# Transposes behind a burst, exponentials held back inside a block, loads held ahead of the sums of x: attention and MLP on one core

## The chip, the cores and the metric

The kernel runs on one core of a Trainium2 chip. The core has five engines with instruction queues of their own: TensorE (PE; PEld is its weight load), VectorE (DVE), ScalarE (ACT), GpSimd (POOL) and SyncE (SP), and 16 DMA engines that all queues share. The metric is the device time in microseconds of one execution, lower being better.

## The reference

Attention over 8 batches, 12 heads, 448 tokens and 64 columns a head, followed by a two-layer MLP on the 3584 x 768 result:

```python
attn = softmax(q @ k.T / sqrt(64))           # per batch and head
x = (attn @ v).transpose(0, 2, 1, 3).reshape(3584, 768)
h = x @ w_in                                  # 768 x 2048
out = maximum(0.01 * h, h) @ w_out            # 2048 x 768, float32
```

All inputs and the output are float32 in HBM; the kernel computes in bf16 with float32 sums.

## The kernel before

**Units, chunks, rows.** A unit is a pair of heads of one batch; there are 48, six to a batch. Its q and k are cast to bf16 (`cast`, lines 164 to 174: on POOL, a tile `qkb` with three buffers) and transposed into `qkT` (four buffers). Units below 15 are transposed on TensorE (`transposes`, eight small transposes at line 268 into a PSUM bank and a VectorE copy at line 274); from unit 15 on, SP issues a DMA transpose (`dma_transposes`, line 251). A unit has four chunks of 112 keys, numbered through (chunk 4u + c). For a chunk TensorE makes the scores of both heads (line 285), ScalarE their exponentials e (line 294). A burst is three chunks in a row, in the three PSUM slots. Rows of a unit (`rows`, line 802) multiply the exponentials by v; VectorE divides (lines 808 and 809) and x is turned into `xT`, by a DMA transpose on SP, or, for units 9, 10 and 11 (`X_PE`), on TensorE by `settle_x` some time later (lines 331 and 332).

**The MLP.** Tokens are worked in seven ranges (`cuts`): 640, 512, 512, 512, 512, 384 and 512. The first range is made in a head (448 tokens, 16 blocks of the hidden dimension, numbered from 0; line 366 makes a block in two halves of three matmuls) and a neck (its other 192 tokens, line 662, which take the k-steps of the first two groups except the last before anything else). Each block ends in a Prelu on ScalarE into h (lines 642 and 687). Two PSUM banks, taken in turn by `next_bank`, serve the blocks and the transposes. The later ranges are made by `hidden` (line 483), which works with sums and differences of x and of the weights: `mix_x_part` (line 430, VectorE) makes those of x, in place and in `x_mix`, in two parts, once the rows that they need have been turned. `second(i)` multiplies h of range i by `w_out` (lines 555 and 620), joins on VectorE (lines 560 and 563) and stores. Between its matmuls it places the bursts and rows for later ranges, and the sums of x of the next range, on VectorE's queue too.

**What sets the order.** All engines run what the program writes in the order in which it is written; nothing is moved at run time. Head, neck and `second` call a planner, `place`, with a small model of TensorE's time (`now`), of ScalarE's (`act`) and of when each slot is free. At each step it may place a due transpose, a burst (if all three slots will be free), or rows. In head and neck a step is called full when a block has just been closed, and not full when half of one is done. `lazy` is the number of a burst's exponentials that are not issued at once but after the next block's Prelu (`settle`); no rows are placed while such ones are owed. Behind a burst of head and neck, `feed` places POOL's casts and loads.

In `second` and `hidden`, `advance` places at each of its steps a DMA transpose, a cast of q and k, a cast of v and a load, as far as each may go. A load (`load_soft`, line 143) fetches two units of one of q, k and v by a DMA that POOL issues and that casts on the way; a load from unit u may go once unit u - 3, the last one in the buffer that it overwrites, has been cast. Before the change it is tried at every second step (`tick`). `mix_x_part`'s first part is placed from 7 us of the model behind the last row but one that the next range needs, the second part 7 us behind the last one (`fresh`, `summed`).

Of the kernel before, what the change touches and what calls it, by code (L numbers as in the profile page):

```python
# [16 lines left out]
def kernel(  # L17
# [16 lines left out]
    NSC = S // SC  # L34
# [3 lines left out]
    NU = B * HP  # L38
# [610 lines left out]
    def neck(outs):  # L649

        n = cuts[1] - HEAD
        at = place_of(HEAD)
        ms = [x + y for x in range(0, MH, 2) for y in (0, MH)]
        held = {}

        def part2(m, kks):
            fresh = m not in held
            if fresh:
                held[m] = next_bank()
            for j in range(2):  # L660
                for kk in kks:
                    nc.tensor.matmul(  # L662
                        held[m][:, j * n:(j + 1) * n], w_in_sb[:, kk, ts(m + j, P)], xT[:, kk, at:at + n],
                        start=(fresh and j == 0 and kk == 0), stop=(kk == KD - 1), skip_group_check=True,
                    )

        assert all(u == need[1] - 1 for u, _ in owed_x), owed_x
        def after(x):
            for _ in range((0, 0, 2, 3, 4, 3, 0, 0)[x]):
                next(outs)  # L670

        for m in ms[:2]:
            part2(m, range(KD - 1))
        yield 4 * (KD - 1) * n / 2400, False
        for x, m in enumerate(ms):
            if x < 2:
                assert rows_done >= need[1], rows_done
                settle_x()
                part2(m, (KD - 1,))
                if x:  # L680
                    after(x - 1)
            else:
                part2(m, range(KH))
                after(x - 1)
                yield 2 * KH * n / 2400, False
                part2(m, range(KH, KD))
            nc.scalar.activation(
                h[:, m:m + 2, HEAD:cuts[1]], held.pop(m)[:, :2 * n].rearrange("p (m t) -> p m t", m=2), AX.Prelu, alpha=0.01
            )
            settle(1)  # L690
            yield 2 * (KH if x > 1 else 1) * n / 2400, True
        model["free"][id(slots[0])] = model["now"] + 1.5
        transposes(NPE - 1, next_slot()[:, 0])
        after(len(ms) - 1)
# [71 lines left out]
    chunk = 4 * HP + 3  # L766
    rows_done = HP
    to = {"pe": HP + 2, "turn": NPE, "q": HP + 4, "cast": HP + 4, "v": HP + 4, "load": [HP + 8] * 3}
    tick = 0

    def advance():
        nonlocal tick
        tick += 1
        u = to["turn"]
        if u < min(NU, chunk // NSC + NQ, to["cast"]):
            dma_transposes(u)
            to["turn"] += 1
        u = to["cast"]
        if u < min(NU, to["turn"] + 2, to["load"][0], to["load"][1]):
            cast(u, (0, 1))  # L780
            to["cast"] += 1
        u = to["v"]
        if u < min(NU, rows_done + NV, to["load"][2]):
            cast(u, (2,))
            to["v"] += 1
        if tick % 2 == 0:
            x = min(range(3), key=lambda x: to["load"][x])
            u = to["load"][x]
            if u < NU and u - 3 < (to["cast"], to["cast"], to["v"])[x]:
                load_soft(u, 2, (x,))  # L790
                to["load"][x] += 2
# [42 lines left out]
    X_PE = (HP + 3, HP + 4, HP + 5)  # L834
    owed_x = []

    def settle_x(now=None):
        while owed_x and (now is None or owed_x[0][1] <= now and model["free"].get(id(slots[0]), 0.0) <= now + 0.05):
            model["free"][id(slots[0])] = model["now"] + 1.0
            model["now"] += 0.3  # L840
            x_transposes(owed_x.pop(0)[0], next_slot()[:, 0])
# [43 lines left out]
    def place(i, want, soon=0, full=True, calm=True, first=False, lazy=0, keen=NU, cap=NU):  # L885

        free, ready = model["free"], model["ready"]
        done, state = 0, 0
        while True:
            settle_x(model["now"])  # L890
            now = model["now"]
            last = divmod(chunk + 2, NSC)[0]
            blocked = rows_done <= min(last, NU - 1) - NE
            u = rows_done
            whole = u < chunk // NSC
            at = [free.get(id(x), 0.0) for x in slots]
            u = to["pe"]
            if full and max(want, soon) > done and u <= min(last, NPE - 1) and state == 0:
                transposes(u)
                to["pe"] += 1  # L900
                state = 1
                model["now"] += 0.45
                continue
            if want > done and state < 2 and turned(last) and not blocked and len(slots) == 3 and all(
                x <= now + 0.05 + 0.2 * j for j, x in enumerate(at)
            ):
                state = 2
                order = list(slots)
                start = chunk
                burst(lazy)  # L910
                if first:
                    feed(start // 3)
                done += 1
                for x, t in enumerate(order[:chunk - start]):
                    model["act"] = max(model["act"], now + 0.45 + 0.2 * x) + 0.8
                    free[id(t)] = model["act"] + (0.3, 0.15 + 0.5 * (lazy > 1), 0.15 + 0.5 * lazy)[x]
                    if (start + x) % NSC == NSC - 1:
                        ready[(start + x) // NSC] = model["act"] + 0.1
                model["now"] = now + 0.78
                continue  # L920
            u = to["pe"]
            if first and full and state == 0 and u < min(NPE - 1, to["cast"] - 1) and u <= chunk // NSC + 1 and model["act"] <= now + 0.6:
                transposes(u)
                to["pe"] += 1
                state = 1
                model["now"] += 0.45
                continue
            u = rows_done
            if calm and whole and not (lazy and late) and at[0] <= now + 0.05 and ready.get(u, 0) <= now + 0.05 and (
                u <= (chunk + 5) // NSC - NE or u < keen  # L930
            ) and u < cap:
                t = slots[0]
                rows()
                if first:
                    pay()
                model["now"] = now + 1.08
                free[id(t)] = now + 2.33
                continue
            return done

    def second(i):

        x_sums = [mix_x_part(i + 1, slice(0, 2)), mix_x_part(i + 1, slice(2, 3))] if i + 1 < NR else []
        fresh, summed = [None, None], [i + 1 == NR] * 2
        left = plan[i]
        for c in range(len(spots(i)[1])):
            whole = c < plain(i)
            for x, _ in enumerate((plain_pair if whole else block_pair)(i, c)):
                fine = 1 if whole else 2
                if x % (2 * fine) == 0:  # L950
                    advance()
                if c or x:
                    model["now"] += 0.65 / fine
                left -= place(i, left, calm=whole or x not in (1, 2), keen=need[min(i + 2, NR)], cap=NU if all(summed) else need[i + 2])
                if whole and x in (1, 3, 5, 7):
                    mix_h(i, x - 1)
                if whole and x in (8, 9, 11, 13, 15):
                    next(outs)
                if i == 0 and c and x % 4 == 2:
                    next(ins, None)  # L960
                for y in range(2):
                    if fresh[y] is None and i + 1 < NR and rows_done >= need[i + 2] - 1 + y:
                        fresh[y] = model["now"] + 7.0
                for y, todo in enumerate(x_sums if x % fine == 0 else ()):
                    if fresh[y] is not None and fresh[y] <= model["now"] and not summed[y]:
                        summed[y] = next(todo, 0) is not None
                        if not summed[y]:
                            break
# [10 lines left out]
    for steps, aims, cost in ((head(ins), early, 0.55), (neck(outs), goals, 0.5)):  # L979
        groups = 0  # L980
        base = len(early) if aims is goals else 0
        for used, full in steps:
# [2 lines left out]
                groups += 1  # L985
                model["act"] = max(model["act"], model["now"]) + cost
            soon = base + sum(x <= groups + 1 for x in aims) - done if full else 0
            done += place(0, base + sum(x <= groups for x in aims) - done, soon, first=True, lazy=2 if aims is goals else 1, full=full, keen=NU if aims is goals or groups > 14 else 0)
    settle()
    assert done == len(early) + len(goals), (done, chunk, rows_done)  # L990
    assert to["pe"] == NPE - 1, to
# [5 lines left out]
    for _ in outs:  # L997
        pass
    for i in range(1, NR):
        for step, _ in enumerate(hidden(i)):  # L1000
            advance()
            if step % 4 == 2 and NSC * (rows_done + 1) <= chunk:
# [33 lines left out]
```

## Time and profile before

| what | value |
|---|---|
| time, median of 3 runs | 387.25 us (386.56 to 387.47) |
| the profiled execution | 387.23 us, span 385.4 us |
| TensorE busy | 375.7 us, 97% of the span |
| ScalarE busy | 264.2 us, 69% |
| VectorE busy | 234.1 us, 61% |
| POOL busy | 141.7 us, 37% |
| exponentials (line 294) | 192 of 920 ns |
| loads of q, k, v in the steady part | 57 of 224 KB, 5.6 to 7.0 us to landing (medians) |
| DMA transposes into qkT, into xT | 33 and 45, 4.4 and 4.9 us to landing (medians) |

Stages on TensorE's timeline: first units to 25.7 us, head to 64.2, neck to 75.2, `second(0)` to 107.6, then `hidden` and `second` by turns, the last scores at 334, the last matmul at 381.4.

A line of a timeline gives start, duration, engine, source line, operation, what is written and read, shapes and count; in brackets the idle time before it and what ended it. A line of the waits gives the waiting engine and line, what it waited for, the sum in us, how often, and the longest. A line of the chain gives start, duration and what was running on the path that ended last. The ends of matmuls are modelled, so distances are taken from start to start.

### The profile page before, as it was taken

To read this page: it belongs to the slowest core of one execution; us is meant where nothing else is said; L and a number is where in the kernel's file an instruction comes from. 1 tells how busy PE (TensorE), PEld (TensorE's weight loads), DVE (VectorE), ACT (ScalarE), POOL (GpSimd) and SP (SyncE) were. 2 spreads that over 40 slices of the span, in tenths; PEclk is the share of its full clock that TensorE was granted. 3 is DMA by queue.
4 is the path that set the end of the run, shared out by engine and by line. 5 is a ranking of instruction groups with operands and counts; after the bars stand their busy time and mean duration, and the time that the engine had idled before them with its cause. 6 is when DMAs were issued, how large, how long until landed. Compare 5 with 4: busy or idle time off the path is not lost.

```text
span 385.4 us, 10023 instructions
## 1 busy us (share of the span) xinstructions
PE 375.7 (97%) x4095; PEld 260.0 (67%) x4095; DVE 234.1 (61%) x488; ACT 264.2 (69%) x391; POOL 141.7 (37%) x223
## 2 busy tenths in 40 slices
PE   8999989999999999999999999999999999999995
PEld 3664646866488655886568865678655895668753
DVE  3663656775666746757459574566745665474753
ACT  5996874865768777687775877767776687717700
POOL 5998660764655443440436304353042100000000
PEclk9999999999999999999999999999999999999999
DMA  8999999899989948991499913999229600330022
GB/s 160 181 195 202 179 193 204 95 135 179 166 149 124 153 72 156 194 156 26 65 182 189 138 26 54 181 173 164 29 46 180 144 13 3 107 80 27 3 83 82
DMA packets 93278, 47.09 MB, mean 122 GB/s; under 512 B 51888, under 2 KB 89904, under 8 KB 93232
## 3 DMA queue, kind: packets, MB, share of 16 engines
q0 software_dynamic: 37536, 22.24, 45.5%
q1 hardware_dynamic: 55056, 23.66, 32.0%
q8 instruction: 32, 0.52, 0.6%
q10 hardware_dynamic: 640, 0.56, 0.5%
q14 instruction: 14, 0.11, 0.1%
HBM read 45.61 MB, written 11.01 MB: 147 GB/s over the span
## 4 chain that ended last, share of the span: by engine, by line
PE 90%; ACT 4%; DMA 2%; DVE 1%; issue 1%; ACTq 0%; DVEq 0%
PE g L555 30%; PE g L483 14%; PE sc L483 14%; PE sc L285 10%; PE sc L802 10%; PE g L366 3%; ACT e L294 3%; PE g L620 3%; PE g L662 2%; DMA xT<-x 2%; PE g L268 1%; DMA hmix<-in_k_dram 1%; PE g L304 1%; PE sc L366 1%; PE g L331 0%
## 5 line engine op out<-in xcount | busy, mean ns | idle before, releaser
L294 ACT ACTIVATE e<-sc 112x896 bf16<-112x896 f32 x192 | 162.7, 920 | 47.7 <-PE sc L285 47.7
L555 PEld LDWEIGHTS <-h 128*128 128x128 bf16 x632 | 57.2, 98 | 45.4 <-issue 13.7
L555 PE MATMUL g<-w_out_sb,h 128*128 128x384 bf16 x416 | 81.0, 326 | 0.0
L472 ACT ACTIVATE h<-c 128x512 bf16<-128x512 f32 (+1 forms) x72 | 43.5, 611 | 25.8 <-DVE c L498 17.4
L483 PEld LDWEIGHTS <-w_in_sb 128*128 128x128 bf16 x576 | 54.3, 98 | 5.9
L285 PE MATMUL sc<-qkT 64*128 64x448 bf16 x384 | 50.0, 355 | 1.4 <-ACT e L294 0.6
L172 POOL COPY qkb<-fq 112x512 bf16<-112x512 bf16 x38 | 25.4, 668 | 68.8 <-DMA qkT<-qkb 33.7
L174 POOL COPY v<-fv 112x512 bf16<-112x512 bf16 x38 | 24.6, 660 | 69.2 <-PE sc L802 69.2
L802 PEld LDWEIGHTS <-e 112*128 112x128 bf16 x1344 | 46.2, 97 | 5.0 <-ACT e L294 0.8
L802 PE MATMUL sc<-v,e 112*128 112x65 bf16 x1344 | 47.6, 193 | 0.4 <-ACT e L294 0.4
L483 PEld LDWEIGHTS <-w_in_mix 128*128 128x128 bf16 x432 | 41.2, 98 | 4.1
L560 DVE COPY o<-g 128x384 f32<-128x384 f32 x49 | 27.1, 554 | 21.6 <-PE g L555 21.3
L555 PE MATMUL g<-w_mix,h 128*128 128x384 bf16 (+1 forms) x208 | 38.3, 323 | 0.9 <-DVE o L563 0.9
L285 PEld LDWEIGHTS <-qkT 64*128 64x128 bf16 x384 | 15.6, 94 | 28.3 <-issue 19.5
L172 POOL COPY qkb<-fk 112x512 bf16<-112x512 bf16 x38 | 25.8, 678 | 19.4 <-DMA fk<-in_k_dram 19.4
L808 DVE RECIPROCAL rec<-sc 112x8 f32<-112x8 f32 x42 | 8.7, 207 | 39.2 <-PE sc L802 39.1
L563 DVE TENSOR_TENSOR o<-o,g 128x384 f32<-128x384 f32 x39 | 21.5, 552 | 17.4 <-PE g L555 15.6
L809 DVE TENSOR_TENSOR x<-sc,rec 112x512 bf16<-112x512 f32 x42 | 29.0, 691 | 1.4
L483 PE MATMUL g<-xT,w_in_sb 128*128 128x256 bf16 (+1 forms) x216 | 28.5, 268 | 0.0
L483 PE MATMUL sc<-xT,w_in_sb 128*128 128x256 bf16 (+1 forms) x216 | 28.5, 268 | 0.0
L555 PE MATMUL g<-w_mix,hmix 128*128 128x384 bf16 x104 | 20.1, 326 | 0.0
L366 PE MATMUL g<-xT,w_in_sb 128*128 128x448 bf16 x84 | 18.7, 353 | 1.3 <-ACT h L642 1.3
(106 smaller groups left out, 478.5 us busy)
## 6 DMA issues: line engine op xcount, KB each, us to landing
fq<-in_q_dram POOLq DMA_DIRECT2D x19, 224.0 KB, 5.6
fk<-in_k_dram POOLq DMA_DIRECT2D x19, 224.0 KB, 7.0
fv<-in_v_dram POOLq DMA_DIRECT2D x19, 224.0 KB, 5.7
w_in_sb<-in_moe_w_in_dram POOLq DMA_DIRECT2D x4, 768.0 KB, 11.3
w_out_sb<-in_moe_w_out_dram POOLq DMA_DIRECT2D x4, 768.0 KB, 19.2
out_dram<-o SPq DMA_DIRECT2D x7, 336.0 KB, 4.7
out_dram<-o SPq DMA_DIRECT2D x8, 288.0 KB, 4.0
out_dram<-o SPq DMA_DIRECT2D x7, 240.0 KB, 3.7
```

The source lines that it names most:

```text
L172: by(qk_sb[u][:, x].rearrange("p so h d -> p h so d"), f)
L174: by(v_sb[u % NV][:, :, :, :D], f)
L285: nc.tensor.matmul(ps[:, j, :S], t[j * D:(j + 1) * D, S + c * SC:S + c * SC + P], t[j * D:(j + 1) * D, :S], start=True, stop=True,)
L294: nc.scalar.activation(e[:, :, c, :], sc_t.pop((u, c))[:SC, :, :S], AX.Exp, scale=scale)
L366: nc.tensor.matmul(open_t[m][:, :n], w_in_sb[:, kk, ts(m, P)], xT[:, kk, at:at + n], start=(fresh and kk == kks[0]), stop=(kk == KD - 1),)
L472: nc.scalar.activation(hs[:, m:m + 2, cols], x.rearrange("p (m t) -> p m t", m=2), AX.Prelu, alpha=0.01)
L483: nc.tensor.matmul(ps[:, j * nh:(j + 1) * nh], w[:, kk, ts(j, P)], x[:, kk], start=(first and j == 0 and kk == 0), stop=(kk == KH - 1), sk ...
L555: nc.tensor.matmul(ps[:, cols], x[:, m], w[:, m], start=(first and m == 0), stop=(m == MH - 1), skip_group_check=True,)
L560: by(o[:, at], ps[:, :NW])
L563: nc.vector.tensor_add(o[:, at], o[:, at], ps[:, :NW])
L802: nc.tensor.matmul(ps[:, j, qc, :D + 1], e[:, at:at + P], vt[:, j, c, :D + 1], start=(c == 0), stop=(c == NSC - 1),)
L809: nc.vector.tensor_mul(x_t[u].rearrange("p q j d -> p j q d"), ps[:SC, :, :, :D], rec.to_broadcast([SC, 2, NSC, D]))
```

## The change

Four edits. In head and neck, directly behind a burst placed at a full step, the next unit's transposes follow if the next burst will need that unit (`soon_due`); the older condition stays beside it, and both now also ask that the `qkT` buffer is free. In head, a burst placed at a step that is not full issues one exponential at once and two later (`lazy` 2 instead of 1); in the neck it was 2 already. Ahead of the neck, an assertion on the x still to be turned becomes a call that turns those of units below the range's last one. And `advance` tries a load at every step, except while `hold` is set: in `second`, from the last row but one that the next range needs until both parts of its sums have been placed.

```diff
-        assert all(u == need[1] - 1 for u, _ in owed_x), owed_x
+        settle_x(last=need[1] - 1)
...
-    tick = 0
+    hold = False
 
     def advance():
-        nonlocal tick
-        tick += 1
...
-        if tick % 2 == 0:
+        if not hold:
             x = min(range(3), key=lambda x: to["load"][x])
...
-    def settle_x(now=None):
-        while owed_x and (now is None or owed_x[0][1] <= now and model["free"].get(id(slots[0]), 0.0) <= now + 0.05):
+    def settle_x(now=None, last=NU):
+        while owed_x and owed_x[0][0] < last and (now is None or owed_x[0][1] <= now and model["free"].get(id(slots[0]), 0.0) <= now + 0.05):
...
             u = to["pe"]
-            if first and full and state == 0 and u < min(NPE - 1, to["cast"] - 1) and u <= chunk // NSC + 1 and model["act"] <= now + 0.6:
+            soon_due = state == 2 and u <= (chunk + 2) // NSC
+            if first and full and u < min(NPE - 1, to["cast"] - 1) and u - NQ < chunk // NSC and (
+                soon_due or state == 0 and u <= chunk // NSC + 1 and model["act"] <= now + 0.6
+            ):
                 transposes(u)
...
                 if x % (2 * fine) == 0:
+                    hold = i + 1 < NR and rows_done >= need[i + 2] - 1 and not all(summed)
                     advance()
...
-            done += place(0, base + sum(x <= groups for x in aims) - done, soon, first=True, lazy=2 if aims is goals else 1, full=full, keen=NU if aims is goals or groups > 14 else 0)
+            done += place(0, base + sum(x <= groups for x in aims) - done, soon, first=True, lazy=2 if aims is goals or not full else 1, full=full, keen=NU if aims is goals or groups > 14 else 0)
...
     for i in range(1, NR):
+        hold = False
         for step, _ in enumerate(hidden(i)):
```

More of the change, by code (lines that the diff above doesn't have):

```diff
@@ L941, in second @@
     def second(i):
+        nonlocal hold
         x_sums = [mix_x_part(i + 1, slice(0, 2)), mix_x_part(i + 1, slice(2, 3))] if i + 1 < NR else []
```

## The prediction

> **What bounds the kernel now.** I read the page's busy shares first, then the waits, then the chain and the timelines of the two places that the edits touch.
>
> ```profile
> PE 375.7 (97%) x4095; PEld 260.0 (67%) x4095; DVE 234.1 (61%) x488; ACT 264.2 (69%) x391; POOL 141.7 (37%) x223
> ...
> PEclk9999999999999999999999999999999999999999
> DMA  8999999899989948991499913999229600330022
> ```
>
> TensorE is busy for 97% of 385.4 us at full granted clock, so only its remaining waits can be won. The DMA engines are at eight or nine tenths up to 106 us (eleven slices of 9.6 us): a transfer moved there meets others. The waits from 30 us to 76 us, then from 76 us to 110 us:
>
> ```profile
> PE g L366 <- ACT h L642: 1.3, 2, 0.9
> ...
> PEld L802 <- ACT e L294: 0.6, 1, 0.6
> ```
> ```profile
> DVE x_mix L430 <- DMA xT<-x: 1.8, 1, 1.8
> ...
> PE g L555 <- DVE o L563: 0.9, 1, 0.9
> ...
> PEld L285 <- DMA qkT<-qkb: 0.3, 1, 0.3
> ```
>
> These are all of TensorE's avoidable waits but some tenths. The first two lie in the head, at 35.31 and 51.51; TensorE's timeline of both:
>
> ```profile
> 33.13 1.31 PE L366 MATMUL g<-xT,w_in_sb 128*128 128x448 bf16 x6
> 34.28 0.56 PE L268 MATMUL g<-c,qkb 112*128 112x112 bf16 x8
> 35.31 1.86 PE L366 MATMUL g<-xT,w_in_sb 128*128 128x448 bf16 x9 [0.48 <-ACT h L642]
> ...
> 50.09 0.56 PE L268 MATMUL g<-c,qkb 112*128 112x112 bf16 x8
> 51.51 1.86 PE L366 MATMUL g<-xT,w_in_sb 128*128 128x448 bf16 x9 [0.86 <-ACT h L642]
> ```
>
> Eight transposes take the one free bank, and the next block must have the bank whose Prelu (h) is queued on ScalarE behind exponentials. From start to start, eight transposes take 0.40 us and three block matmuls 0.62 us (the chain), so the losses are 0.64 and 1.03 us. The third place, on the chain:
>
> ```profile
> 98.36 0.18 issue
> 98.55 0.14 DVE w_in_sb L405
> 98.68 5.84 DMA xT<-x
> ...
> 105.05 0.47 DVE o L563
> 105.52 0.04 issue
> 105.56 0.48 PE g L555 x2
> ```
>
> The transpose of row 16's x is issued at 98.68 and lands at 104.53; VectorE stands at the first sum and, behind it in order, at the join that TensorE needs. TensorE could have gone on at 104.53 and does at 105.56: 1.03 us. The remaining line, 0.3 us of weight load at 84.02, matters most below: the first score on unit 15 starts when its DMA transpose lands (issued 76.60, 7.4 us to landing). TensorE ends its earlier work there at 84.08, so this costs nothing now, but there is no slack at all. From 108 us to the last scores no wait but the fixed cadence of the scores shows, so the loads can win nothing there.
>
> **The change, part by part.** The profiled execution took 387.23 us (span 385.4 and 1.8 around it), 0.02 below the median 387.25; I sum against 387.23.
>
> *Unit 8's transposes.* The same eight transposes and VectorE copy, now behind chunks 27 to 29 instead of behind block 3. Followed through the planner by its own numbers, this is the only case: elsewhere the next burst does not need the unit yet. Burst at 32.27, next matmul 33.13, transposes to 33.53, block 3 to 34.77, block 4 there instead of at 35.31: -0.54 us. Unit 8's cast was done long before, and the copy has 1.2 us until block 4 needs the bank.
>
> *Two exponentials late instead of one, in bursts inside a block.* At 51.51 h then waits behind one exponential: it starts at 50.12 and ends at 50.67, against 51.46, and block 11 starts 0.79 us earlier. In the other such bursts ScalarE waits some 0.1 us for the block's end before h, covered by slots that are free 0.3 us ahead.
>
> *What the planner does with it.* It books the third slot 0.5 later (0.15 + 0.5 x lazy). After chunks 39 to 41 that gives 19.89 + 1.15 = 21.04 against a limit of 20.51 + 0.45 = 20.96: chunks 42 to 44 go from the middle of block 12 to its end, 45 to 47 from the middle of block 14 to its end, rows 10 and 11 from the middle of block 15 behind it. The wait in row 11 for its last exponential (61.71, 0.6 us) keeps some 0.4, the one before x of row 9 (57.36, 0.3) some 0.2: -0.3 together. But the transposes of x of row 10 come straight before the neck's first matmuls, of which the fifth needs them. VectorE must first normalise row 11: 0.27 from TensorE's end to the reciprocal, 0.21, 0.69 and 0.38 us of copy, 1.6 with the hand-overs, against 0.20 of transposes and 4 x 0.082 on TensorE: +1.1 us. Row 11's x is turned only behind those 20 matmuls; the next two need it: 0.51 from its start to VectorE, 0.38, 0.06, less 0.20: +0.75 us. Today both hide under block 15 and the 20 matmuls. Chunks 48 to 50 then miss their slot by 33.33 against 33.24 and go one group later, chunks 51 to 53 half a block later, which spares the 0.19 us before 69.09. Settling x ahead of the neck finds nothing below row 11: zero. Head and neck: -0.54 - 0.79 - 0.3 - 0.19 + 1.1 + 0.75 = 0.0, between -0.5 and +0.4 by how the hand-overs fall.
>
> *Why a gain there would not last.* Unit 15's transpose waits for POOL, whose order of casts and loads is unchanged and which starts at 68.09, when q of unit 14 lands 17.8 us after its issue, weights queued ahead of it. That load, POOL's ten steps up to 76.57 and the 7.4 us do not depend on TensorE. If TensorE comes 0.5 us earlier, it waits 0.5 us at 84.02. So this part counts 0, with -0.1 and +0.4 as ends.
>
> *Loads at every step.* No load is added; each costs POOL 0.70 us of issue and blocks the casts behind it. In range 0 POOL is behind the written order, held by landings:
>
> ```profile
> 87.02 0.70 POOL L143 DMA_DIRECT2D fq<-in_q_dram  x1
> ...
> 91.83 0.61 POOL L172 COPY qkb<-fq 112x512 bf16<-112x512 bf16 x1 [2.31 <-DMA fq<-in_q_dram]
> 95.09 0.61 POOL L172 COPY qkb<-fk 112x512 bf16<-112x512 bf16 x1 [2.65 <-DMA fk<-in_k_dram]
> ...
> 97.38 0.70 POOL L143 DMA_DIRECT2D fv<-in_v_dram  x1
> ...
> 100.86 0.70 POOL L143 DMA_DIRECT2D fq<-in_q_dram  x1
> 101.55 0.70 POOL L143 DMA_DIRECT2D fk<-in_k_dram  x1
> ```
>
> Worked on in the new order, units 20's q and k are loaded at 85.3 and 87.3 (now 87.02, 88.82), then v of 20 at 94.4, q, k and v of 22 at 96, 98 and 100 (now 97.38, 100.86, 101.55, 110.43), q and k of 24 at 105. Unit 18's casts slide 0.2 us; SP's order of transposes and stores is the same, so row 16's x is still issued at 98.7. The rule "no loads" is written from row 16 on, but at POOL those loads, allowed steps before, are only then being issued. So the transpose of row 16 still meets loads all along. Its price from both sides: 2.4 us, what a transpose with no load in flight took (185.5), would end the wait, -1.03; 7.7 us, the unit-20 transpose issued at 96.57, would add 1.9. Nearest is row 17's, in the same stretch with two loads in flight: 6.0 against 5.84. I take +0.2.
>
> The Trainium skill, page "DMA: Bandwidth & Descriptors", section "Queues, rings and completion order", says that each DMA engine goes round the queue rows that have work, one packet at a time. By that rule a second load behind a first takes no further share, and the sum stays at +0.2. The same page, section "Latency and other measured facts", gives 0.2 us for a memory access on average and 2 us under high load; by that, an estimate would add up to 1.8 us instead. No row here separates the two.
>
> *Holding loads in ranges 1 to 5.* One or two loads of 4 to 6 us leave the stretch before the sums and go before it or into the next range. Nothing waits for a landing there; the shortest lead of a transposed unit over its scores is 3.5 us (unit 26, landed 150.40, used 153.91), and the held loads are cast a whole stage later. Zero: even at 7.7 us unit 26 would land at 153.1, unit 44 (the next shortest, issued 292.14, used 300.16) at 299.9. The other end is a gain of nothing, since no wait is there to end, and a loss of the tenths by which 8 us would miss.
>
> Sum: 0.0 + 0.2 + 0.0: 387.23 + 0.2 = 387.4 us.
>
> **The rivals.** *Loads crowd row 16's x (slower).* At 7.7 us it lands at 106.4 and TensorE goes on at 107.4: +1.9, 389.1 us. It decides from 7.0 us on. For it: one more load (v of 22) falls into a stretch where transposes already took 5.1 to 7.7 us. Against: loads are in flight there now too.
>
> *Unit 17 becomes late (slower).* Issued at 85.28 it took 3.1 us with no load beside it and is used at 91.50; now q of 20 is issued in the same instant. At 7.4 us, as unit 15's took, it lands at 92.7: +1.2, 388.4 us. It starts to cost at 6.2 us.
>
> *The hold works, unit 15 still pins.* Row 16's x lands by 103.5: -1.03, 386.2 us. Against it speaks POOL's backlog.
>
> *Hold and head both count (faster).* Unit 15 lands 0.5 us earlier, say because the 1.04 us of POOL's unexplained idling before 73.07 is gone, and row 16's wait ends: -1.5, 385.7 us.
>
> **How the numbers follow.** The forecast has 0.38 (own range 386.7 to 388.1), the hold alone 0.10: together 0.48 within 0.3%, 1.16 us, about what a measurement of this kernel tells from no change. Crowding 0.20, unit 17 late 0.08, and 0.06 for a shift in the head or a later range that costs over 1.2 us: 0.34 slower. Both counting: 0.18 faster. The range 385.7 to 389.1 takes in all the named cases.
>
> **What would show it.** Block 4 starting right behind block 3 and a wait of at most 0.3 us before block 11 confirm the head; waits of about 1 and 0.7 us at the fifth neck matmul and before the neck's last k-step confirm its price. A weight load that waits for unit 15's qkT by the amount of TensorE's lead confirms the pin. A first sum of x in range 0 that still waits 1 to 3 us for xT confirms that the hold comes too late. If unit 15 lands before 83.5, or row 16's x takes under 4 us, I am wrong to the fast side; over 7 us, to the slow side.

## The result and the profile after

The changed kernel takes 392.75 us (median of 4 runs, 391.29 to 394.39), the kernel before on the same chip 387.36 us (386.56 to 388.10): a ratio of 1.0141, with a 95% interval from 1.0096 to 1.0186. It is slower by 5.4 us; the forecast was 387.4 us and its upper end 389.1.

The profiled execution took 392.76 us with a span of 391.0 us, 5.5 us more than the one of before. From the page of the kernel after, the busy shares, the granted clock and the DMA engines in 40 slices of 9.8 us:

```profile
PE 377.7 (97%) x4095; PEld 260.8 (67%) x4095; DVE 232.2 (59%) x488; ACT 264.9 (68%) x391; POOL 143.0 (37%) x223
...
PEclk9999999999989999999999999999999999999999
DMA  7999999799999129898297953989229510321022
```

TensorE does the same work. What is new is the 8 in the row of the clock, in the slice from 107.5 to 117.3 us. The DMA engines are as full as before, at eight or nine tenths nearly throughout up to 127 us. The waits from 76 to 114 us (waiting engine, tile and line, what ended the wait, sum in us, how often, longest; the last two lines are the same waits, seen at the weight load and at the matmul):

```profile
DVE x_mix L430 <- DMA xT<-x: 3.5, 1, 3.5
...
PE g L555 <- DVE o L563: 2.6, 1, 2.6
...
PEld L285 <- DMA qkT<-qkb: 2.3, 2, 1.4
...
PE sc L285 <- DMA qkT<-qkb: 1.7, 2, 1.0
```

Before, the three waits of VectorE and TensorE were 1.8 (x_mix), 0.9 (g of line 555) and 0.3 us (qkT, at the weight load). All three have grown, and they lie in the same place: while `second(0)` runs. Set against each other on TensorE's own timeline, start to start, the lag of the kernel after grows in these steps:

| TensorE's work | before, at | after, at | lag | step |
|---|---|---|---|---|
| first scores | 6.39 | 6.86 | 0.48 | 0.48: first loads landed later |
| first product of `second(0)` | 75.20 | 75.38 | 0.18 | -0.30: head and neck |
| first score on unit 15 | 84.02 | 85.28 | 1.26 | 1.08: unit 15's qkT |
| burst at chunk 66 | 91.11 | 93.20 | 2.09 | 0.83: unit 16's qkT |
| burst at chunk 78 | 105.98 | 109.85 | 3.87 | 1.78: sums of x |
| last product of range 1's `hidden` | 127.91 | 133.36 | 5.45 | 1.58: clock |
| hidden of the last range | 344.55 | 350.00 | 5.45 | 0.0 |

Behind 133 us nothing is lost or won. The steps at units 15 and 16 on TensorE's timeline:

```profile
85.28 0.74 PE L285 MATMUL sc<-qkT 64*128 64x448 bf16 x6 [1.01 <-DMA qkT<-qkb]
...
89.03 0.55 PE L285 MATMUL sc<-qkT 64*128 64x448 bf16 x4 [0.66 <-DMA qkT<-qkb]
```

The chain of the kernel after through the step of the sums (start, duration, what ran):

```profile
101.71 6.59 DMA xT<-x
...
108.39 0.53 DVE x_mix L430
108.92 0.47 DVE o L563
...
109.43 0.48 PE g L555 x2
```

It is the same chain as before, 3.9 us later: row 16's x is issued 3.03 us later and takes 0.75 longer, VectorE stands at the first sum, the join behind it waits, and TensorE with it. Then the timeline of TensorE:

```profile
109.43 0.48 PE L555 MATMUL g<-w_mix,h 128*128 128x384 bf16 x2 [2.65 <-DVE o L563]
...
110.53 1.73 PE L555 MATMUL g<-w_mix,h 128*128 128x384 bf16 x6
112.05 1.49 PE L483 MATMUL g<-xT,w_in_sb 128*128 128x256 bf16 x6
113.33 1.33 PE L483 MATMUL sc<-xT,w_in_sb 128*128 128x256 bf16 x6
...
115.47 0.82 PE L483 MATMUL g<-xT,w_in_sb 128*128 128x256 bf16 x6
```

Six matmuls of line 483 take 0.82 us at 115.47, as before, but 1.49 and 1.33 at 112.05 and 113.33. Granted clock and DMA share in three stretches (in each row the length, then PE, PEld, DVE, ACT and POOL, then the clock, the DMA share, above 1 where packets of several queues overlap, and GB/s):

```profile
109.00:112.00 3.00, 2.57 (x14) 1.07 (x14) 2.23 (x5) 1.68 (x3) 1.65 (x3) 0.82 1.29 189
112.00:115.00 3.00, 3.00 (x30) 2.28 (x29) 2.25 (x5) 1.74 (x4) 1.87 (x4) 0.61 0.93 232
115.00:118.00 3.00, 3.00 (x45) 2.74 (x42) 2.09 (x4) 0.98 (x3) 3.00 (x6) 1.00 0.78 150
```

The records of the clock put it at one half from 111.0 to 114.4 us, 3.4 us that begin 1.5 us after TensorE took up work again. The mean clock over the span was 0.993 to 0.996 in all four runs of the kernel after, and 1.000 in the profiled one of before.

The head went as the prediction had it. TensorE's timeline at blocks 3 and 4, where the wait of 0.48 us is gone, and in the neck, where the two new ones stand:

```profile
33.62 0.57 PE L268 MATMUL g<-c,qkb 112*128 112x112 bf16 x8
34.02 2.25 PE L366 MATMUL g<-xT,w_in_sb 128*128 128x448 bf16 x11
...
64.02 1.48 PE L662 MATMUL g<-xT,w_in_sb 128*128 128x192 bf16 x16 [0.86 <-DVE xT L332]
...
66.18 0.49 PE L662 MATMUL g<-xT,w_in_sb 128*128 128x192 bf16 x4 [0.48 <-DVE xT L332]
```

### The profile page after: what moved, and what is told of

It reads as the page before. It is cut to its first block, busy times and chain, and to the rows that moved or that the text cites. A ratio compares the mean times of both kernels' runs of the same rounds, so it can differ in the third digit from the quotient of the medians.

```text
span 391.0 us, 10020 instructions
## 1 busy us (share of the span) xinstructions
PE 377.7 (97%) x4095; PEld 260.8 (67%) x4095; DVE 232.2 (59%) x488; ACT 264.9 (68%) x391; POOL 143.0 (37%) x223
## 4 chain that ended last, share of the span: by engine, by line
PE 71%; DMA 19%; POOL 7%; issue 1%; DVE 0%; SPq 0%; POOLq 0%; DVEq 0%
PE g L555 29%; PE g L483 14%; PE sc L483 14%; DMA fq<-in_q_dram 9%; PE sc L800 7%; PE sc L285 7%; POOL qkb L172 3%; DMA w_mix<-in_q_dram 2%; DMA qkT<-qkb 2%; DMA xT<-x 2%; DMA fk<-in_k_dram 2%; POOL v L174 1%; DMA w_in_mix<-in_v_dram 1%; DMA hmix<-in_q_dram 1%; POOL fq L143 1%
## 5 line engine op out<-in xcount | busy, mean ns | idle before, releaser
L172 POOL COPY qkb<-fq 112x512 bf16<-112x512 bf16 x38 | 27.0, 712 | 65.7 <-DMA qkT<-qkb 39.8
L483 PE MATMUL g<-x_mix,w_in_mix 128*128 128x256 bf16 (+1 forms) x144 | 19.0, 268 | 0.0
```

Of the source, the lines that this page charges most:

```text
L172: by(qk_sb[u][:, x].rearrange("p so h d -> p h so d"), f)
L483: nc.tensor.matmul(ps[:, j * nh:(j + 1) * nh], w[:, kk, ts(j, P)], x[:, kk], start=(first and j == 0 and kk == 0), stop=(kk == KH - 1), sk ...
```

## The experiments

Three readings compete. **Loads**: the loads at every step carry the loss, by crowding the transposes in `second(0)`. **Head**: the edits of head and neck carry it, by what they shift downstream. **Clock**: part of it is no wait at all, but the half clock behind one. Ratios are to the kernel before, run on the same chip (387.0 to 387.6 us in the median). The waits are those of one profiled execution of each kernel.

### Each part alone

The edits of head and neck alone (the diff without its lines on `tick` and `hold`):

> The edits of head and neck alone; loads at every second step and no hold, as before. Theory A (the loads carry the loss): the waits for x of rows 10 and 11 in the neck stay (1.0 and 0.6 us), unit 15 still pins TensorE near 84 to 85 us, but row 16's x in range 0 waits about 1.0 us as before and the clock is not cut: 387.0 to 388.5 us. Theory B (the head edits bring TensorE into the DMA-bound stretch at a worse moment and carry most of the loss): over 390 us, with the waits at units 15 and 16 and at the sums as in the kernel after.

Measured: 387.67 us, ratio 1.0001 (0.9981 to 1.0020). The neck's waits are there, 0.86 and 0.48 us of idling as after, and the sums keep TensorE idle nowhere by more than some tenths. So the head alone is not the loss.

The two edits of the loads alone:

```diff
-        if tick % 2 == 0:
+        if not hold:
...
+                    hold = i + 1 < NR and rows_done >= need[i + 2] - 1 and not all(summed)
                     advance()
```

> The edits of the loads alone: a load at every step, held ahead of the sums; head and neck as before. Theory A: the wait for row 16's x grows from 1.0 to 2 to 3 us and the granted clock is cut to a half for about 3 us behind it (1.5 us lost): 389.5 to 392 us. Theory B: 387 to 388 us, the wait at the sums about as before.

Measured: 392.08 us (388.63 to 395.75), ratio 1.0092 (1.0052 to 1.0133). Its profiled execution, 388.63 us, is the fastest of the eight, and has the wait of the sums without the half clock:

```profile
DVE x_mix L430 <- DMA xT<-x: 2.7, 1, 2.7
...
PE g L555 <- DVE o L563: 1.9, 1, 1.9
```

Of its eight runs, the two with a mean clock of 0.999 took 388.6 and 390.2 us, all others, at 0.994 or less, 391.5 us or more. So the loads carry the larger part of the loss, by the ratios 0.9% of 1.4%, with intervals that overlap; the clock is a step in it that some runs take and some do not. Single runs of other kernels have such a clock too, the kernel before among them (391.05 us at 0.995).

Loads at every step, with `hold` never set:

```diff
-        if tick % 2 == 0:
+        if not hold:
```

> Loads at every step and never held; the rest as before. If the hold comes too late in range 0, since POOL then still issues loads that were allowed steps before, this is within 0.5 us of the load edits with the hold. If the hold protects the sums, this is 1 us or more slower than the load edits with the hold, in range 0 or in later ranges.

Measured: 394.73 us, ratio 1.0146 (1.0092 to 1.0200). Row 16's x takes 9.2 us to landing, TensorE idles 4.2 us, and the half clock lasts 6.8 us; one of the four runs took 390.62 us, with the clock at 1.000. The median is 2.65 us above that of load_edits, the expectation's second case, though the two intervals overlap. Its transpose among the DMA issues, its wait, and the clock in two stretches:

```profile
xT<-x SPq DMA_TRANSPOSE x1, 9.2
```
```profile
PE g L555 <- DVE o L563: 4.2, 1, 4.2
```
```profile
109.00:112.00 3.00, 1.76 (x8) 0.39 (x7) 2.67 (x4) 0.38 (x1) 2.90 (x5) 0.51 1.04 129
112.00:115.00 3.00, 3.00 (x13) 1.51 (x12) 1.64 (x5) 2.15 (x3) 0.61 (x1) 0.50 1.40 224
```

The hold at the old pace (`hold` is set as in the change; only the line that reads it is shown):

```diff
-        if tick % 2 == 0:
+        if tick % 2 == 0 and not hold:
```

> Loads at every second step as before, and the hold added. If pulling the loads forward does the harm, this is 386.3 to 387.6 us, with a wait for row 16's x of 0 to 1.0 us. If the hold itself did the harm, 389 us or more.

Measured: 387.56 us, ratio 1.0001 (0.9982 to 1.0021). TensorE does not wait for the sums of range 0 (VectorE 1.2 us, all covered). The hold does ease that wait: with a load at every step TensorE idles 1.9 us with it and 4.2 without, at the old pace not at all with it and 0.9 without. Alone it wins nothing that shows in the time; units 15 and 16 cost TensorE 0.9 us in that execution (here and below from start to start, less the 0.26 or 0.20 us that the step takes without a wait).

### Where the loads cost

The changed kernel with the old pace in `second(0)` alone:

```diff
-        if not hold:
+        if not hold and (late_pace or tick % 2 == 0):
...
+    late_pace = True
     for i in range(1, NR):
```

> The changed kernel, but in second(0) alone a load is tried at every second step again (the hold stays everywhere, and from range 1 on every step has its load). Theory: all of the loss is made while second(0) runs, where GpSimd is behind its written order and each earlier load pushes the casts and the transposes back. Then the time is that of the kernel before, 387.4 us (386.5 to 388.4), units 15 and 16 make TensorE wait under 0.8 us together, the sums of range 0 under 1.2 us, and the granted clock stays full. Rival: the loads at every step also cost in the later ranges, or the edits of head and neck cost once they meet the hold: 389 us or more, with the waits behind 112 us or at units 15 and 16 as in the changed kernel.

Measured: 388.06 us, ratio 1.0013 (0.9987 to 1.0039). The 0.5 us that are left of the loss lie within the uncertainty: it is made in `second(0)`, and loads at every step in the later ranges cost nothing that can be measured while the hold stands. (Without it, in every_step_no_hold, TensorE idled 0.69 us at 215.8 us for the sums of range 3.) One number of the expectation was missed: units 15 and 16 cost TensorE 1.4 us, not under 0.8. Row 16's x:

```profile
xT<-x SPq DMA_TRANSPOSE x1, 3.8
```

The changed kernel with the hold of range 0 set three rows earlier:

```diff
-                    hold = i + 1 < NR and rows_done >= need[i + 2] - 1 and not all(summed)
+                    hold = i + 1 < NR and rows_done >= need[i + 2] - (1 if i else 4) and not all(summed)
```

> The changed kernel, with the hold of range 0 set from the row of unit 13 on instead of from that of unit 16: v of unit 20 and all of units 22 and 24 are loaded only behind the sums; q and k of unit 20 still go at every step. Theory: what costs in range 0 is that these loads run beside the transposes of the rows' x and of units 19 to 21. Without them the transpose of row 16's x takes 3.8 to 5.8 us, as in the traces at the old pace (6.6 to 9.2 in those with a load at every step), and SyncE needs 11.2 to 11.6 us from the issue of unit 18's transpose to that of row 16's x (11.3 to 13.0 with them). The sums' wait costs TensorE under 1.2 us, the clock stays full: 387.0 to 388.5 us. Unit 17's transpose still takes 5.4 to 5.9 us, since q of unit 20 is issued with it. Rival: the loss comes from GpSimd's order ahead of that, at units 15 to 18: 389.5 us or more.

Measured: 388.10 us, ratio 1.0040 (1.0010 to 1.0069), as the theory had it. The sums cost TensorE nothing and the clock stays full in the profiled execution; one of the ten runs, 392.39 us, had a mean clock of 0.993. The transposes of row 16's x, and of unit 17, which still has q of unit 20 issued with it:

```profile
xT<-x SPq DMA_TRANSPOSE x1, 4.5
```
```profile
qkT<-qkb SPq DMA_TRANSPOSE x1, 6.3
```

What is left are the waits for units 15, 16 and 17 (0.87, 0.39 and 0.22 us) and 0.6 us of idling behind the sums of the next range. So the hold of the change is right in kind and comes too late in range 0, where GpSimd is that far behind its written order.

The kernel before with nothing moved, and transfers added that nobody reads:

```diff
                     advance()
+                    if i == 0 and c == 1 and x in (0, 8):
+                        for y in (q, k):
+                            t = c_pool.tile([P, 4 * P], F32, name="c")[:SC]
+                            nc.scalar.dma_start(
+                                out=t.rearrange("p (h x) -> p h x", h=2),
+                                in_=y[x // 8, 2:4].rearrange("h (p so) d -> p h (so d)", so=NSC),
+                            )
```

> The kernel before, with its order untouched, and four transfers of 229 KB more that ScalarE issues in second(0) (two at the first step of its last pair of blocks, two at the third) and that nobody reads; no load of q, k or v is moved and GpSimd and SyncE do what they did. Theory: it is the crowding of the DMA engines alone that lengthens the transposes. Then row 16's x or unit 20's transpose, whichever runs beside them, takes 7 us or more (5.8 and 7.7 before), the sums' wait on TensorE grows from 1.0 to 2 to 4 us, and the time to 388.5 to 391 us. Rival: only GpSimd's and SyncE's order matters, and transfers beside each other take each other nothing: row 16's x takes 3.8 to 5.8 us, and the time stays at 387 to 388 us.

Measured: 391.05 us (two runs), ratio 1.0104 (1.0066 to 1.0142), but this time must not be read as the theory's. ScalarE, which issues the added transfers, stood 3.8 us ahead of an exponential behind them, and TensorE waited for that exponential, not for the sums:

```profile
103.95 1.43 PE L802 MATMUL sc<-v,e 112*128 112x65 bf16 x32 [3.24 <-ACT e L294]
```

What can be read are the transfers themselves. Row 15's x, issued between the first two added transfers, took 7.7 us against 4.9 before; unit 21's transpose, with the last two behind it, 9.8 against 5.1; unit 19's 7.8 against 5.9. In the other thirteen traces these three took 3.0 to 5.9, 3.0 to 8.6 and 3.6 to 6.2 us. Row 16's x, issued at 99.82 when the first of the added ones was about to land, took 5.2 against 5.8, so the expectation missed the row that it named. The two pairs of this kernel, then of before:

```profile
xT<-x SPq DMA_TRANSPOSE x1, 7.7
...
qkT<-qkb SPq DMA_TRANSPOSE x1, 9.8
```
```profile
xT<-x SPq DMA_TRANSPOSE x1, 4.9
...
qkT<-qkb SPq DMA_TRANSPOSE x1, 5.1
```

The written order on GpSimd and SyncE was untouched here: transfers beside a transpose lengthen it by themselves.

The other traces together point the same way. Row 16's x, by the number of loads of q, k and v that were in flight 1 us after its issue:

| loads in flight | kernels | us to landing |
|---|---|---|
| none | loads_behind_the_sums | 4.4 |
| one | before, head_edits, range0_old_pace, heads_kept_order, v_behind_unit_16, hold_early | 5.8, 5.4, 3.8, 5.2, 5.4, 4.5 |
| two | hold_old_pace, after | 5.0, 6.6 |
| three | load_edits, fill_the_wait, sums_later | 7.5, 6.8, 7.2 |
| four | every_step_no_hold | 9.2 |

One caution: row 16's x is issued 1.3 to 3.2 us behind unit 20's transpose, and in none of the fourteen traces did it land ahead of it; in six it landed within 0.8 us behind. So part of the time that the table counts for it may be unit 20's, and no run here separates the two.

### The clock

The changed kernel, with idle products where TensorE stood still:

```diff
+        if i == 0 and c == len(spots(0)[1]) - 1:
+            for _ in range(12):
+                nc.tensor.matmul(slots[0][:, 0], w_out_sb[:, 0, :P], w_out_sb[:, 1, :512], start=True, stop=True)
         yield from product(b, h[:, hi, two], t4)
         keep(o2, left, b)
```

> The changed kernel, with twelve idle products of 512 columns (weights by weights, into the PSUM slot that is next in turn, read by nobody; some 2.5 us of TensorE) placed just ahead of the last product of range 0's last block, where TensorE stood idle for 2.8 us. The output is unchanged. Theory: it is the idle stretch that is followed by half the granted clock, which cost some 1.6 us behind it. Filled, the clock stays full from 109 to 116 us and the time is 1.6 us below the changed kernel's 392.75: about 391.2 us (390.3 to 391.9). Rival: the clock falls for another cause (the load of the stage, its place in time): the slices behind 111 us still show half the clock, and the time stays at 392.7 or above.

Measured: 390.76 us, ratio 1.0072 (1.0046 to 1.0099), 2.0 us below the median of the kernel after; by the ratios it is 2.7 us, with intervals that just touch. The mean clock of its four runs was 0.997 to 1.000, against 0.993 to 0.996. VectorE still waited 3.3 us for row 16's x, so the cause of the wait is untouched; but the clock is full from 10.4 to 385.9 us, and the six matmuls of line 555 take 1.15 us again instead of 1.73 (line 606 is that of the idle products):

```profile
105.39 2.75 PE L606 MATMUL sc<-w_out_sb 128*128 128x512 bf16 x11
107.98 0.49 PE L555 MATMUL g<-w_mix,h 128*128 128x384 bf16 x2
...
109.08 1.15 PE L555 MATMUL g<-w_mix,h 128*128 128x384 bf16 x6
110.06 0.82 PE L483 MATMUL g<-xT,w_in_sb 128*128 128x256 bf16 x6
```

So it is the idle stretch that brings the half clock, which costs 1.6 us on top of the wait in the profiled execution of the kernel after.

The changed kernel with its sums 2 us of the model later:

```diff
-                        fresh[y] = model["now"] + 7.0
+                        fresh[y] = model["now"] + 9.0
```

> The changed kernel, with the sums of x placed from 9 us of the model behind the rows instead of 7, in every range. Theory: in range 0 VectorE does not stand at the first sum with a join behind it for which TensorE waits; the wait for row 16's x then falls behind that join. The wait of 2.8 us shrinks to 0 to 1.0 and the half clock behind it is gone: 392.75 - 1.8 to 2.8 - 1.6 = 388.4 to 389.4, and up to 1 us is given back if the first products on the sums then wait: 388.4 to 390.4 us. Rival: the wait only moves, to the start of hidden of range 1, which needs the same sums, and the idle stretch and its clock come back there: 392 us or more.

Measured: 390.28 us, ratio 1.0086 (1.0058 to 1.0114). In the profiled execution the wait of line 555 is gone and the clock full, although row 16's x took 7.2 us; 1.2 us of it come back at the start of `hidden` of range 1, which waits for the join behind the sums:

```profile
DVE x_mix L430 <- DMA xT<-x: 2.4, 1, 2.4
...
PE g L483 <- DVE o L563: 1.2, 1, 1.2
```

In range 3 the later sums cost another 1.1 us (line 483, at 209 us), so this is no remedy for every range.

### What the head would be worth

The head's edits with the planner's bookings as before (`book` is 1 in the head where `lazy` has become 2), the old pace, and in `feed` the loads behind the casts:

```diff
-                    free[id(t)] = model["act"] + (0.3, 0.15 + 0.5 * (lazy > 1), 0.15 + 0.5 * lazy)[x]
+                    free[id(t)] = model["act"] + (0.3, 0.15 + 0.5 * (book > 1), 0.15 + 0.5 * book)[x]
...
                 to[y] = u + 4 + r
-                fetch(1)
```

> The kernel before, with the old pace of the loads and no hold. Unit 8's transposes go early and two exponentials are late inside a block of the head, as in the change, but the planner books the slots as for one late exponential, so that bursts 42 and 45 and the rows of units 10 and 11 stay where they were; and in feed the loads of unit 18 go behind the casts of unit 15 instead of between them. Theory: the head gains 0.5 and 0.8 us (blocks 4 and 11), the neck's waits for x of rows 10 and 11 (1.0 and 0.6 us) do not appear, and the transpose of unit 15 is issued some 1.0 us earlier, so that its landing no longer takes the gain away: 387.2 - 1.0 to 1.4 = 385.8 to 386.2 us. Rival: the gain is taken by the next landing, unit 16's or row 16's x, whose issue hangs on GpSimd and not on TensorE: 386.9 to 387.6 us, with a wait for qkT of unit 16 or for the sums of about 1 us longer than before.

Measured: 387.14 us, ratio 0.9986 (0.9970 to 1.0001). The head gave 1.08 us against the kernel before (counted from the burst at chunk 27 to the neck), no wait stands in the neck, and unit 15's transpose, issued at 76.01, landed at 80.48 instead of 83.97. But unit 16's took 7.95 us and landed at 87.86, 1.6 us later than before, and cost TensorE 1.15 us, more than the head had given: the rival's case. The sums cost nothing, row 16's x having been issued 1.6 us earlier.

On top of that, v of unit 18 loaded behind unit 16's casts (`n` is how many loads `fetch` may issue):

```diff
-        pay()
+        pay(2 if g == 16 else 3)
...
-            fetch()
+            fetch(0 if g == 16 else 3)
```

> As heads_kept_order, but v of unit 18 is loaded behind the casts of q and k of unit 16 instead of ahead of them. Theory: the 1.3 us that TensorE waited there for unit 16's transpose (7.95 us beside three loads just issued) were the next landing that took the gain; issued 0.7 us earlier and beside two loads it lands by 86 us and TensorE waits 0.4 us at most. Unit 18 is cast no later, so row 16's x comes as in heads_kept_order and the sums cost nothing: 1.1 us from the head and 1.0 us from the sums remain, 387.4 - 2.1 + 0.0 to 0.4 = 385.3 to 385.7 us. Rival: unit 16's transpose still takes 7 to 8 us, or row 16's x comes later: 386.3 to 387.3 us.

Measured: 387.14 us, ratio 0.9998 (0.9975 to 1.0021). Unit 16's transpose was issued 1.5 us earlier and landed 0.4 us later: 9.9 us. It cost TensorE 1.66 us. The rival again.

And on top of that, fewer loads in `second(0)`: v of unit 18 behind the casts of unit 19, and none from the row of unit 13 until the sums (the lines that leave it out of `fetch` are not shown):

```diff
-        if tick % 2 == 0:
+        if tick % 2 == 0 and not hold:
...
+                    hold = i == 0 and rows_done >= need[2] - 4 and not all(summed)
                     advance()
+                    if i == 0 and c == 0 and x == 6:
+                        load_soft(18, 2, (2,))
```

> As v_behind_unit_16, but the old pace goes with a hold in range 0 alone, from the row of unit 13 until the sums are placed, and v of unit 18, which no row needs before 108 us, is loaded only in second(0), behind the casts of unit 19. So one load fewer runs beside the transposes of units 15 and 16, and v of unit 20 and units 22 and 24 do not run beside those of row 16's x. Theory: the DMA engines are full from 76 to 106 us, and what is gained anywhere is lost again at the next landing unless bytes leave that stretch. With a load of 224 KB gone, unit 16's transpose lands by 86.5 us instead of 87.9 to 88.3 and TensorE waits under 0.5 us there; row 16's x takes 4 to 5 us and the sums cost nothing: 387.2 - 1.1 (head) - 1.0 (sums) + 0 to 0.5 = 385.1 to 385.6 us. Rival: unit 16's transpose is held by its place in SyncE's queue, behind that of row 12's x, and lands at 87.5 us or later all the same: 386.3 to 387.3 us.

Measured: 386.23 us (385.46 to 390.17) against 387.01, ratio 0.9986 (0.9959 to 1.0013). By the ratios it is 1.5% (6.0 us) below the changed kernel, and by the medians 0.8 us below the one of before, which its interval does not separate from no change; the median lies between the theory's range and the rival's. Row 16's x took 4.4 us and the sums cost nothing; unit 16's transpose landed at 86.72, between the two expectations, and TensorE idled for it:

```profile
86.77 0.55 PE L285 MATMUL sc<-qkT 64*128 64x448 bf16 x4 [0.60 <-DMA qkT<-qkb]
```

What holds unit 16's transpose stays open. It lands at 85.9 to 89.0 us in all fourteen traces, whether issued at 78.4 or at 82.1, and always behind row 12's x, which SyncE issues just ahead of it; that one or the bytes of the loads beside it could be the cause, and no run here tells them apart.

## Why the prediction was wrong

**Head and neck: right.** Unit 8's transposes gave 0.64 us (forecast 0.54, with block 3 taken at 1.24 us, where the timeline of before shows 1.15), block 11 came 0.63 us earlier (0.79), the neck's waits came at 64.02 and 66.18 with 1.02 and 0.64 us from start to start (1.1 and 0.75), and the sum of head and neck was -0.30 (0.0, between -0.5 and +0.4). head_edits confirms that it does not show in the time.

**The pin at unit 15: right in kind, wrong in size.** TensorE's lead was lost there, but the term "0, with -0.1 and +0.4 as ends" took the landing at 83.97 for fixed. Over the traces in which `feed` is unchanged it lies between 83.0 and 85.3 us, with a transpose of 6.7 to 7.75 us. In the kernel after it landed at 85.23 and cost 1.08 us: 0.30 is the head's gain, lost there as forecast, and 0.78 is a landing later than the shifted start explains. Counted from the first scores it landed as late in hold_old_pace (78.5 us behind them, 78.4 after, 77.6 before), whose program does not differ from the one of before up to there, so this part is the chance of an execution. And the next landing was overlooked: behind a late unit 15, unit 16's (7.5 us against 5.8) cost 0.83 more. That is an execution's chance too: fill_the_wait and sums_later, which are the kernel after up to there, have neither wait, with unit 15 landed at 84.08 and 83.87 and unit 16 at 86.28 and 85.89.

**Row 16's x: the step that failed.** Two halves of it. That "row 16's x is still issued at 98.7" is wrong: it went at 101.71 (at 100.06 in fill_the_wait and 99.06 in sums_later). SyncE's order is the same, but SyncE issues without a break from unit 18's transpose on, and each transpose occupies it for 1.2 to 2.2 us. From unit 18's issue to that of row 16's x it needs 11.4 us before and 13.0 after; and unit 18's itself starts from unit 15's landing, because GpSimd's first cast of unit 17 starts when that transpose has landed (85.28 behind 85.23). So a landing 1.26 us later moved that whole queue. In the timeline of SyncE, before and then after, row 16's x is the last line; after, VectorE had written it at 98.0:

```profile
94.01 1.37 SPq L251 DMA_TRANSPOSE xT<-x  x1
95.47 1.00 SPq L344 DMA_DIRECT2D out_dram<-o  x2
96.57 2.02 SPq L251 DMA_TRANSPOSE qkT<-qkb  x1
98.68 1.29 SPq L251 DMA_TRANSPOSE xT<-x  x1
```

```profile
95.83 1.28 SPq L251 DMA_TRANSPOSE xT<-x  x1
97.20 2.16 SPq L344 DMA_DIRECT2D out_dram<-o  x2
99.46 2.16 SPq L251 DMA_TRANSPOSE qkT<-qkb  x1
101.71 1.26 SPq L251 DMA_TRANSPOSE xT<-x  x1
```

Of the 1.7 us by which that queue ran longer, 1.2 is one store of the output, which occupied SyncE for 1.69 us instead of 0.53. Stores nearly as long stand in that place in fill_the_wait and sums_later (1.39 and 1.50) and in no kernel at the old pace (at most 0.54). What holds such a store stays open, and so does how much of the 1.7 us is due to loads: in the other kernels with a load at every step the same way took 11.3 to 12.2 us, in those at the old pace 10.9 to 12.4.

The other half is the price. "Nearest is row 17's" and "I take +0.2" chose the lower row; with the change's loads and hold it took 6.6 to 7.5 us in four traces, between that row and the unit-20 transpose of 7.7 us. TensorE's wait grew by 1.78 us. 0.75 of it is that price; 0.94 is the later issue, 3.03 us, of which TensorE had itself lost 2.09; the rest is hand-overs. So the number is that of the rival *Loads crowd row 16's x* (+1.9, given 0.20), and its mechanism is less than half of it here; its sign, over 7 us, did not even show in this execution (6.6). load_edits has the mechanism alone: issued at 97.77, it took 7.5 us, and TensorE idled 1.9 us instead of 0.9.

**Loads beside a transpose: a reading that does not hold.** The Trainium skill, page "DMA: Bandwidth & Descriptors", section "Queues, rings and completion order", was read in the prediction as saying that a second load behind a first takes no further share. The table above speaks against that: with three or four loads in flight row 16's x took 6.8 to 9.2 us, with one 3.8 to 5.8. Nor is one load free: unit 17's transpose took 2.9 to 3.1 us in the five kernels at the old pace whose `feed` is unchanged, where it was issued ahead of that load, and 5.4 to 6.3 in the six kernels that issue q of unit 20 with it. The closest pair is hold_old_pace and the kernel after, issued at 86.83 and 86.85 us behind much the same transpose of unit 16: 2.9 and 5.7 us. In before, then in after, in the stretch from 85 to 87.3 us:

```profile
fq<-in_q_dram POOLq DMA_DIRECT2D x1, 224.0 KB, 4.8
qkT<-qkb SPq DMA_TRANSPOSE x1, 3.1
```
```profile
fq<-in_q_dram POOLq DMA_DIRECT2D x1, 224.0 KB, 4.9
qkT<-qkb SPq DMA_TRANSPOSE x1, 5.7
```

That is the rival *Unit 17 becomes late* by half: it landed at 92.55, some 1 us before its use, and cost TensorE 0.2 us in hold_early alone. The load itself lost nothing (4.8 and 4.9 us).

**The clock: a term that was missing.** The forecast priced a wait at its length. Its row PEclk had only nines, with a longest idle stretch of 0.87 us on TensorE in this part, so nothing in the trace of before showed what a longer one does. It cost 1.58 us in the profiled execution.

**The hold: right in the main.** That "the hold comes too late" in range 0 is confirmed by hold_early, though it eases the wait there (4.2 us without it, 1.9 with it), and ranges 1 to 5 are worth nothing, as said.

The steps of the table, added to the time before, give 387.23 + 0.48 - 0.30 + 1.08 + 0.83 + 1.78 + 1.58 = 392.7 us, against 392.76 in the profiled execution. Of these, the sums and the clock, 3.4 us, are the steps that the experiments tie to the loads; load_edits lost 0.9%, or 3.6 us, by its ratio. The start and units 15 and 16 are this execution's, and what makes up the rest of the 1.4% over all runs stays open.

## What to carry to other kernels

Where the DMA engines are full, a transfer that is issued earlier is paid for by whichever transfer the next stage waits for: count what is in flight when that one is issued, and keep what is needed late out of the stretch rather than spread evenly over it. A landing that has no slack is not a fixed time: look for the next landing behind it, and for the queues that start from it, because they move with it. A wait of TensorE that nears 3 us is dearer than its length; work that nobody needs can save the clock behind it, though not the wait itself.

## What the runs showed of the hardware

An idle stretch of TensorE of 2.65 us was followed by 3.4 us at half clock (after), one of 3.24 us by 3.4 (more_traffic), one of 4.19 us by 6.8 (every_step_no_hold); one of 1.91 us by none (load_edits). The half clock began 3.0 to 4.2 us behind the start of the idling, before work was resumed in one case and 0.7 and 1.5 us after it in the others. In all fourteen traces a stretch of full or half clock lasts a whole number of steps of 3.41 us (one, two, 29, 30 and so on), apart from the cut at the end. So it may also matter where an idle stretch lies between two steps; no run here varies that. The Trainium skill, page "TensorE: Matmul & The Clock Gate", section "HAM oscillation — how this bites in real kernels", warns of gaps over some 3.4 us; here 2.65 us were enough, and the measurement decides.

In all fourteen traces the 78 transposes that SyncE issues landed in the order of issue, also where one of them took twice as long as the next; unit 16's landed 0.6 to 3.5 us behind row 12's x.

The start of an execution alone varies: the burst at chunk 27, which all kernels reach with the same program, begins between 31.8 and 33.3 us in the fourteen profiled executions. That spread is as large as the gains that head and hold could bring.
